# A mixture-of-experts kernel: two 64-row remainder units with raw fp32 weights in place of two 128-row units with split weights

## The chip, the cores and the metric

The kernel runs on one core of a Trainium2 chip. The metric is the time of one execution on the device in microseconds (us); the median of 3 runs before is 899.38 us. The engines are named as in the profile: PE (matmul), PEld (PE's weight loads), DVE (vector), ACT (scalar), POOL (GpSimd) and SP (which issues most DMAs).

## What is computed

Attention over 4 x 448 rows of 12 heads of 64, then two mixture-of-experts layers over the 1792 rows of 768. Each layer sends every row to one of 8 experts and multiplies it by that expert's two matrices, in fp32:

```
for e in range(E):                       # E = 8
    mask = e_idx == e                    # argmax of the gate's logits
    if not mask.any():
        continue
    h = np.maximum(x[mask] @ w1[e], 0.0) # 768 x 1024
    out[mask] = gate_w[mask, None] * (h @ w2[e])   # 1024 x 768
```

## The kernel before, in words

The work of a layer is cut into units: some rows of one expert, with a fixed capacity. The second layer is e2, e3, then four units of up to 304 rows in `seq` (B0 to B3, the list `S["B"]`), then two remainder units of up to 128 rows, S0 and S1 (`S["S"]`). Which expert and which rows a unit has is worked out on the device: `table2` and `table3` fill entries, `M.reg` loads them into registers. An expert gets a further 304-row unit while more than 128 rows are left (the threshold `thr`), and a remainder unit for what is left then. If there are more units than these, a branch (`others`, in the middle of B3) does them; it also runs for no unit, and then costs only its test.

A unit is `unit` and `halves` (from line 373). The first half has KF=8 blocks of 128 hidden columns with KD=6 weight tiles of 128x128 each, the second half KD=6 blocks with KF=8 tiles each. Full precision comes from split planes: an fp32 weight `r1[k]` or `r2[k]` becomes an fp16 high plane (`w1h`, `w2h`, a cast on ACT, L294) and a bf16 low plane (`w1l`, `w2l`, a subtraction on DVE, L295). The rows are split in the same way (`xsplit`, L340 and L341) and transposed by DMA (`xtrans`, L344). `mm3` (L357) then issues three matmuls per weight tile; the middle one takes its width from a register (`width`, at least 32), so the profile writes it as 128x0:

```
for (ah,al,bh,bl) in pairs:
    for o,a,b in ((p,ah,bh),(s(p),ah,s(bl)),(p,al,bh)):
        self.nc.tensor.matmul(o,a,b,start=i==0,stop=i==tot-1); i+=1
```

The relu makes `hh` (ACT, L360) and `hl` (DVE, L361). The second half's results are copied (L424), transposed on PE (`ytrans`, L414), multiplied by the gate (DVE, L415) and scattered to the output by POOL (L366); the last block's are done at the start of the next unit (`post`).

The work for later units is woven in. At step 0 the unit fetches the payload (row numbers and gates) of the unit after next, at step 7 its rows (a gather on POOL, L336). In the first half `split_w2` makes this unit's w2 planes. At step 7.5 the next unit's w2 is loaded into `r2`. In the second half `warm2` splits the next unit's w1, and behind it `bring` loads the w1 of the unit after next into `r1`. `XPLAN` says when the next unit's rows are split and transposed. The program order of each engine is pinned (`pin`).

Of the kernel before, what the change touches and what calls it, by code (L numbers as in the profile page):

```python
# [27 lines left out]
class Moe:  # L28
# [287 lines left out]
    def fetch_pay(self,u,slot=None):  # L316
        nc=self.nc
        if slot is None: u.slot=self.slot; self.slot=(self.slot+1)%4
        s=self.reg(u.ent,u.g,1,E*NT-1)
        pay=self.pays[u.slot]; N=u.N; ordt=u.L.ord  # L320
        FT=N//128; rem=N-FT*128
        nc.sync.dma_start(out=pay[:,:FT,:],in_=ordt[ds(s,FT*128),:].rearrange("(t p) w -> p t w",p=128))
# [9 lines left out]
    def gather(self,u,t=None):  # L332
        nc=self.nc; ntl=u.ntl; idx=self.idxs[u.slot]
        for t in range(ntl) if t is None else (t,):
            m=u.rows[t]
            nc.gpsimd.indirect_dma_start(out=self.xr[t][:m],out_offset=None,in_=u.L.src[0:u.nrow,:],in_offset=bass.IndirectOffsetOnAxis(ap=idx[:m,t:t+1],axis=0),bounds_check=u.nrow-1,oob_is_err=False)  # L336
    def xsplit(self,u,t,eng=None,part=2):

        nc=self.nc; m=u.rows[t]; x=self.xr[t][:m]; h=self.XS[:m,t,0]
# [33 lines left out]
    def unit(self,u,nx=None,fx=None,side=None,late=0,mid=None,fast={},now=False,fp=0,fr=7,**kw):  # L373

        gen=self.gen(); side=dict(side or {})
        plan=XPLAN[late] if nx is not None else {}
        def do(s):
            if fx is not None and s==fp: self.fetch_pay(fx)
            for k,t in plan.get(s,()):
                if t<nx.ntl:  # L380
                    if k=="t": self.xtrans(nx,t)
                    else: self.xsplit(nx,t,self.nc.gpsimd if k=="p" else None)
            if fx is not None and s==fr: self.fetch_rows(fx)
            for _ in range(fast.get(s,1)): next(gen,None)
            for f in side.pop(s,()): f()  # L385
        warm=nx is not None and not nx.same
        for _ in self.halves(u,nx,warm,do,fx,cut=mid is not None,**kw): mid([k for s in plan if s<MID for k in plan[s]])
        for _ in gen: pass
        for s in sorted(side): do(s)
        if now:  # L390
            self.flush()
            if fx is not None: self.fetch_idx(fx)
        elif fx is not None and fr>KF+KD: self.fetch_rows(fx)
    def halves(self,u,nx,warm,do,fx=None,early=True,wfb=None,gp=0,cut=False):
# [17 lines left out]
        def ytrans(d):  # L412
            q=self.pt.tile([128,4,128],F32,name="pty",tag="pt")[:,:ntl]
            for t in range(ntl): nc.tensor.transpose(q[:,t,:],self.yt[:,d,ts(t,128)],self.ident)  # L414
            nc.vector.tensor_tensor(out=self.yr[:,:ntl,ts(d,128)],in0=q,in1=bc(pay[:,:ntl,1:2],[128,ntl,128]),op=ALU.mult)  # L415
        Y={}
        def after(d):
            ytrans(d)
            if u.L.nxt is not None:
                for j in range(2): nc.tensor.matmul(self.lgp[:2*E,:N],u.L.nxt["wgs"][:,d],Y.pop((d,j)),start=(d,j)==(0,0),stop=(d,j)==(KD-1,1))  # L420
        for db in range(KD):
            p=self.ps.tile([128,512],F32,name="pl2",tag="pl")[:,:N]
            self.mm3(p,[(self.w2h[:,k,ts(db,128)],self.w2l[:,k,ts(db,128)],hh[:,k],hl[:,k]) for k in range(KF)],r)
            nc.scalar.copy(self.yt[:,db,:N],p)  # L424
            if u.L.nxt is not None:
                yh,yl=[self.st.tile([128,self.NM],F32R,name=n,bufs=2)[:,:N] for n in ("yh","yl")]
                nc.scalar.copy(yh,p); nc.vector.tensor_tensor(out=yl,in0=p,in1=yh.bitcast(F32),op=ALU.subtract)
                Y[db,0],Y[db,1]=yh,yl
            if db>0: after(db-1)
            if warm: self.warm2(db,None)  # L430
            do(KF+db)
        if fx is not None and early and not fx.same: self.bring(fx)
        def post():
# [2 lines left out]
            if u.L.nxt is not None: yield from self.route2(u,pay[:,:ntl,1:2])  # L436
            yield
        self.post=post
    def redo(self,u,nx,fx,turn,done):
        u.e=None; self.fetch(u,u.slot); self.cold(u); self.xall(u)  # L440
        self.turn=turn-1; next(self.halves(u,None,False,lambda s: None,cut=True))
        if nx is None: return
        self.fetch(nx,nx.slot)
        for k,t in done:
            if t<nx.ntl: (self.xtrans if k=="t" else self.xsplit)(nx,t)
# [25 lines left out]
    2:{7.5:[("s",0),("s",1),("s",2),("t",0),("t",1),("t",2)]},None:{10:[("s",0),("t",0)]}}  # L471
class LazyUnit:
    def __init__(self,S,*key,same=False):
        object.__setattr__(self,"_k",(S,key)); object.__setattr__(self,"same",same)
    def _u(self):
        o,key=object.__getattribute__(self,"_k")
        for k in key: o=o[k]
# [6 lines left out]
class Layer:  # L484
    def __init__(self,w1,w2,src,dst,ordt,nxt=None): self.w1,self.w2,self.src,self.dst,self.ord,self.nxt=w1,w2,src,dst,ordt,nxt
class Unit:
    def __init__(self,L,ent,g,N,same=False):
        self.L,self.ent,self.g,self.N,self.same=L,ent,g,N,same
        self.ntl=(N+127)//128; self.rows=[min(128,N-t*128) for t in range(self.ntl)]; self.e=None; self.slot=None; self.nrow=NT; self.w1=False

# [311 lines left out]
def body_full(tc,q,k,v,g_q,g_k,wg,wog,w1,w2,mod,wg2,bias2,v1,v2,out,stop=False,O=None):  # L802
    nc=tc.nc
    with ExitStack() as ctx:
# [145 lines left out]
        def table2():  # L950
            c,off=cc2,off2; M.reduce_counts(tp,c2,lp,tag="tp",out=c)
            rem=lp.tile([128,E],F32,name="rem"); nc.vector.tensor_tensor(out=rem,in0=c,in1=off,op=ALU.subtract)
            M.nchunks(lp,rem,N2,128,out=nb)
            yield
            yield from M.chunks(S["b2"],lp,nb,off,c,N2,G2)
        def table3():
# [5 lines left out]
            yield from M.chunks(S["s2"],lp,ns,off3,c,128,E)  # L962
# [71 lines left out]
```

## Time and profile before

| | |
|---|---|
| median of 3 runs | 899.38 us (899.12 to 903.18) |
| the profiled execution | 898.82 us |
| its span, first to last instruction | 897.0 us |
| PE busy | 831.3 us, 93% |
| DVE busy | 682.4 us, 76% |
| ACT busy | 527.1 us, 59% |
| mean granted clock of PE | 0.978 |

Busy time is the share of the span in which an engine works; a busy PE need not be PE at its peak. The granted clock is a share of 2.4 GHz, and 0.50 is the lower of its two levels, 1.2 GHz. Times in the rows are counted from the span's start.

### The profile page before, as it was taken

To read this page: it belongs to the slowest core of one execution; us is meant where nothing else is said; L and a number is where in the kernel's file an instruction comes from. 1 tells how busy PE (TensorE), PEld (TensorE's weight loads), DVE (VectorE), ACT (ScalarE), POOL (GpSimd) and SP (SyncE) were. 2 spreads that over 40 slices of the span, in tenths; PEclk is the share of its full clock that TensorE was granted. 3 is DMA by queue.
4 is the path that set the end of the run, shared out by engine and by line. 5 is a ranking of instruction groups with operands and counts; after the bars stand their busy time and mean duration, and the time that the engine had idled before them with its cause. 6 is when DMAs were issued, how large, how long until landed. Compare 5 with 4: busy or idle time off the path is not lost. (4 is left out here: it accounts for less than half of the span.)

```text
span 897.0 us, 23334 instructions
## 1 busy us (share of the span) xinstructions
PE 831.3 (93%) x8881; PEld 652.1 (73%) x8898; DVE 682.4 (76%) x1417; ACT 527.1 (59%) x967; POOL 384.1 (43%) x406
## 2 busy tenths in 40 slices
PE   4699999998899799799999999989999999999986
PEld 1366666665565588677889899888777778876776
DVE  6688889888879875776787888888766667654585
ACT  4577776776667652555555566565545545544473
POOL 5686777776776521321423422434113415312020
PEclk9799999999999899999999999999999999999999
DMA  5578665665566472989487687779677595965671
GB/s 133 126 162 194 154 155 166 167 163 150 128 168 156 120 218 56 275 295 332 94 307 209 219 324 218 246 284 303 189 295 205 205 309 150 331 175 210 218 244 55
DMA packets 143931, 181.84 MB, mean 203 GB/s; under 512 B 73737, under 2 KB 111385, under 8 KB 143809
## 3 DMA queue, kind: packets, MB, share of 16 engines
q1 hardware_dynamic: 135712, 157.45, 59.6%
q0 software_dynamic: 6784, 22.32, 7.8%
q8 instruction: 72, 1.18, 0.6%
q10 hardware_dynamic: 1312, 0.47, 0.2%
q14 instruction: 51, 0.41, 0.2%
HBM read 130.12 MB, written 24.33 MB: 172 GB/s over the span
## 5 line engine op out<-in xcount | busy, mean ns | idle before, releaser
L357 PE MATMUL pl<-XT,w1h 128*128 128x304 f16 (+7 forms) x1620 | 250.3, 263 | 5.4 <-PEq L986 2.2
L357 PE MATMUL pl<-hh,w2h 128*128 128x304 f16 (+7 forms) x816 | 209.6, 269 | 0.2
L357 PE MATMUL pl<-hh,w2l 128*128 128x304 f16 (+7 forms) x816 | 209.2, 268 | 0.0
L357 PE MATMUL pl<-XT,w1l 128*128 128x304 f16 (+7 forms) x810 | 207.8, 269 | 1.3 <-DVE w1l L295 1.3
L357 PE MATMUL pl<-hl,w2h 128*128 128x0 bf16 x816 | 202.6, 255 | 3.3 <-DVE hl L361 3.2
L357 PEld LDWEIGHTS <-w1h 128*128 128x128 f16 x1632 | 149.2, 98 | 29.8 <-issue 6.2
L357 PEld LDWEIGHTS <-w2h 128*128 128x128 f16 x1632 | 148.9, 98 | 24.9 <-issue 1.8
L648 POOL TENSOR_TENSOR plo<-p 128x448 f16<-128x448 f32 x142 | 139.3, 1001 | 50.2 <-ACT p L645 46.8
L295 DVE TENSOR_TENSOR w1l<-r,w1h 128x1024 bf16<-128x1024 f32 x96 | 118.1, 1245 | 37.8 <-ACT w1h L294 37.7
L424 ACT COPY yt<-pl 128x304 f32<-128x304 f32 (+7 forms) x102 | 37.2, 364 | 139.1 <-PE pl L357 138.9
L341 POOL TENSOR_TENSOR XS<-xr,XS 128x768 bf16<-128x768 f32 (+5 forms) x27 | 47.3, 1771 | 165.4 <-ACT XS L340 165.4
L294 ACT CAST w1h<-r 128x1024 f16<-128x1024 f32 x96 | 99.6, 1054 | 0.1
L645 ACT ACTIVATE p<-pst,eb 128x896 f32<-128x896 f32 (+1 forms) x96 | 86.5, 911 | 14.4 <-PE pst L641 13.4
L357 PEld LDWEIGHTS <-w2l 128*128 128x128 bf16 x816 | 80.1, 98 | 17.2 <-issue 4.4
L360 ACT ACTIVATE hh<-pl 128x304 f16<-128x304 f32 (+7 forms) x135 | 50.2, 373 | 71.6 <-PE pl L357 64.1
L658 PE MATMUL av<-vv,p 128*128 128x65 f16 (+1 forms) x768 | 89.7, 199 | 2.0 <-ACT xrow L670 2.0
L357 PEld LDWEIGHTS <-w1l 128*128 128x128 bf16 x816 | 80.1, 98 | 14.7 <-DVE w1l L295 1.6
L658 PEld LDWEIGHTS <-p 128*128 128x128 bf16 (+1 forms) x768 | 73.5, 102 | 21.0 <-issue 15.0
L660 PE MATMUL av<-vv,plo 128*128 128x65 f16 (+1 forms) x768 | 87.9, 196 | 0.6 <-DVE plo L648 0.6
L659 PE MATMUL av<-vv,p 128*128 128x64 f16 (+1 forms) x768 | 88.4, 198 | 0.0
L622 DVE TENSOR_REDUCE m<-psm 128x2 f16<-128x896 f32 x70 | 76.0, 1085 | 8.3 <-PE psm L617 6.7
L295 DVE TENSOR_TENSOR w2l<-raw,w2h 128x768 bf16<-128x768 f32 x64 | 73.1, 1142 | 8.4 <-ACT w2h L294 8.2
(314 smaller groups left out, 1661.5 us busy)
## 6 DMA issues: line engine op xcount, KB each, us to landing
r<-in_moe_w_dram SPq DMA_DIRECT2D x96, 512.0 KB, 9.0
raw<-in_moe_w_dram SPq DMA_DIRECT2D x64, 384.0 KB, 5.9
r2a<-in_moe_w_dram SPq DMA_DIRECT2D x32, 384.0 KB, 7.3
r2b<-in_moe_w_dram SPq DMA_DIRECT2D x32, 384.0 KB, 7.7
T<-Z SPq DMA_DIRECT2D x48, 224.0 KB, 3.2
T<-Z SPq DMA_DIRECT2D x48, 112.0 KB, 3.1
yd<-zero SPq DMA_DIRECT2D x14, 384.0 KB, 3.3
rv<-in_v_dram SPq DMA_DIRECT2D x24, 192.0 KB, 3.8
```

The source lines that it names most:

```text
L294: if part!=1: nc.scalar.copy(h,t)
L295: if part!=0: (eng or nc.vector).tensor_tensor(out=l,in0=t,in1=h,op=ALU.subtract)
L341: if part!=0: (eng or nc.vector).tensor_tensor(out=self.XS[:m,t,1].bitcast(BF16),in0=x,in1=h,op=ALU.subtract)
L357: self.nc.tensor.matmul(o,a,b,start=i==0,stop=i==tot-1); i+=1
L360: nc.scalar.activation(h,p,AF.Relu)
L424: nc.scalar.copy(self.yt[:,db,:N],p)
L622: if t<3: nc.vector.tensor_reduce(m[:,t:t+4:3],p[:,:,:S],axis=AX.X,op=ALU.max,negate=True)
L645: self.nc.scalar.activation(self.d["P",i][:,self.u(kt)],p[:,:nn,:S],AF.Exp,bias=self.eb,scale=0.125)
L648: eng.tensor_tensor(out=self.d["L",i][:,u],in0=P[:,u],in1=self.hi(P)[:,u],op=ALU.subtract)
L658: nc.tensor.matmul(o,hh,w[:,0:65],start=kt==0,stop=False)
L659: nc.tensor.matmul(o[:,0:64],hh,w[:,65:129],start=False,stop=False)
L660: nc.tensor.matmul(o,ll,w[:,0:65],start=False,stop=kt==3)
```

## The change

The two remainder units hold NS=64 rows in place of 128, and the threshold for a further 304-row unit falls from 128 to 64. They run in a new function, `unit32`: one matmul per weight tile, with the raw fp32 weights and the fp32 rows, 64 columns wide; no planes, no register for the width. S0 reads its weights from `r1` and `r2`. S1 has buffers of its own: `x1` is new, `x2` is a view of the planes of w1, which are not read any more when it is loaded. S1's w1 is loaded during B1, its w2 during B3. The rows are transposed on PE (`xtrans32`) in place of the DMA. `ytrans` becomes a method.

```diff
+    def alloc_f32(self,st,n):
+        self.x1=[st.tile([128,F],F32,name=f"x1_{i}") for i in range(KD)]
+        self.x2=[t[:,i].bitcast(F32) for t in (...) for i in range(2)]
+        self.xt32=st.tile([128,KD,n],F32,name="xt32"); self.hh32=st.tile([128,KF,n],F32,name="hh32")
...
-        plan=XPLAN[late] if nx is not None else {}
+        plan=XPLAN[late] if nx is not None and not nx.f32 else {}
...
-            if warm: self.warm2(db,None)
+            if warm and not nx.f32: self.warm2(db,None)
...
+    def xtrans32(self,u):
+        nc=self.nc; m=u.rows[0]
+        q=self.pt.tile([128,4,128],F32,name="ptx",tag="pt")...
+        for k in range(KD): nc.tensor.transpose(q[:,k],self.xr[u.x0][:m,ts(k,128)],self.ident[:m,:m])
+        nc.vector.tensor_copy(self.xt32,q)
+    def unit32(self,u,w1,w2,side={}):
+        nc=self.nc; N=u.N; gen=self.gen()
+        def do(s):
+            next(gen,None)
+            for f in side.get(s,()): f()
+        for fb in range(KF):
+            p=self.ps.tile([128,512],F32,name="pl1",tag="pl")[:,:N]
+            for k in range(KD): nc.tensor.matmul(p,w1[k][:,ts(fb,128)],self.xt32[:,k],start=k==0,stop=k==KD-1)
+            do(fb)
+            nc.scalar.activation(self.hh32[:,fb],p,AF.Relu)
+        for db in range(KD):
+            p=self.ps.tile([128,512],F32,name="pl2",tag="pl")[:,:N]
+            for k in range(KF): nc.tensor.matmul(p,w2[k][:,ts(db,128)],self.hh32[:,k],start=k==0,stop=k==KF-1)
+            nc.scalar.copy(self.yt[:,db,:N],p)
+            if db>0: self.ytrans(u,db-1)
+            do(KF+db)
+        def post():
+            self.ytrans(u,KD-1); self.scatter(u)
+            yield
+        self.post=post
...
-            M.set_caps(CAPS,((128,0),(N2,128),(N2,0)))
+            M.set_caps(CAPS,((128,0),(N2,NS),(N2,0)))
...
-        S["B"]=[Unit(L2,be,g,N2) for g in range(G2)]; S["S"]=[Unit(L2,se,g,128) for g in range(E)]
+        S["B"]=[Unit(L2,be,g,N2) for g in range(G2)]; S["S"]=[Unit(L2,se,g,NS,f32=True,x0=g) for g in range(2)]
...
-        sides={0:{KF+i:[stepper("table3")] for i in range(6)},1:{2:[more]},2:{1:[known]},5:{2:[nc.gpsimd.drain]}}
+        def x1(a,b):
+            M.expert(s1)
+            for k in range(a,b): M.load_w(M.x1,L2.w1,s1.e,k)
+            s1.w1=True; s1.e=None
+        def x2():
+            M.expert(s1)
+            for k in range(KF): M.load_w(M.x2,L2.w2,s1.e,k)
+        sides={0:{KF+i:[stepper("table3")] for i in range(6)},1:{2:[more],4:[lambda: x1(0,3)],6:[lambda: x1(3,6)]},2:{1:[known]},3:{8:[x2],9:[lambda: M.xtrans32(s0)]}}
         for j,u in enumerate(seq):
-            nx,fx=seq[j+1] if j<5 else None,seq[j+2] if j<4 else None
+            nx,fx=(seq+[s0,s1])[j+1:j+3]
             M.unit(u,nx=nx,fx=fx,side=sides.get(j),late=0,mid=others(u,nx,fx) if j==3 else None)
+        M.unit32(s0,M.r1,M.r2,{KF:[lambda: M.xtrans32(s1)]})
+        M.unit32(s1,M.x1,M.x2,{2:[nc.gpsimd.drain]})
```

**PE, where B3 ends and S0 begins.** `pl` is the sum in PSUM, `pty` the transposed results, `XT` the transposed rows, `r_0` to `r_5` the tiles of `r1`. Before:

```order
L357 MATMUL pl_27302<-hh,w2l 128x304
L414 MATMUL pty<-ident,yt 128x128 x3
L350 TENSOR_LOAD s2gw
L350 ISA x2
L351 ISA
L357 LDWEIGHTS w1h
L357 MATMUL pl_27364<-XT,w1h 128x128
L357 LDWEIGHTS w1h
L357 MATMUL pl_27364<-XT,w1h 128x128
L357 LDWEIGHTS w1l
L357 MATMUL pl_27364<-XT,w1l 128x128
```

And with the change:

```order
L361 MATMUL pl_27345<-hh,w2l 128x304
L442 MATMUL pty<-ident,yt 128x128 x3
L456 MATMUL pl_27376<-xt_5621,r_0_70 128x64
L456 MATMUL pl_27376<-xt_5621,r_1_71 128x64
L456 MATMUL pl_27376<-xt_5621,r_2_72 128x64
L456 MATMUL pl_27376<-xt_5621,r_3_73 128x64
L456 MATMUL pl_27376<-xt_5621,r_4_74 128x64
L456 MATMUL pl_27376<-xt_5621,r_5_75 128x64
L442 MATMUL pty<-ident,yt 128x128 x3
```

Three matmuls per tile, each with a weight load of its own, become one fp32 matmul, for which the program holds no separate load; the load of the width goes.

**SP, in B1, between the payload fetch for B3 and the input transposes for B2.** `x_0` to `x_5` are the tiles of `x1`. Before:

```order
L323 DMA pay_83<-o_1128 48x4
L344 DMA_TRANSPOSE XT<-XS 128x12x128 x2
L344 DMA_TRANSPOSE XT<-XS 128x12x48
L298 ISA
L298 DMA raw_114<-in_moe_w_dram 128x768
```

And with the change:

```order
L327 DMA pay_83<-o_1128 48x4
L306 TENSOR_LOAD s2gi
L306 ISA x2
L302 ISA
L302 DMA x_0_5615<-in_moe_w_dram 128x1024
L302 ISA
L302 DMA x_1_5616<-in_moe_w_dram 128x1024
L302 ISA
L302 DMA x_2_5617<-in_moe_w_dram 128x1024
...
L302 DMA x_5_5620<-in_moe_w_dram 128x1024
L348 DMA_TRANSPOSE XT<-XS 128x12x128 x2
```

Six loads of 512 KB and two loads of a register stand ahead of the transposes.

**DVE, from B3's second half into S0.** `yr` are the rows to scatter, `xt` is `xt32`. Before:

```order
L295 TENSOR_TENSOR w2l<-raw_114,w2h 128x768
L415 TENSOR_TENSOR yr<-pty,pay_83 128x3x128
L361 SCALAR_TENSOR_TENSOR hl<-pl_27364,hh 128x128
L295 TENSOR_TENSOR w2l<-raw_114,w2h 128x768
L361 SCALAR_TENSOR_TENSOR hl<-pl_27403,hh 128x128
```

And all that DVE has from there to the end with the change:

```order
L443 TENSOR_TENSOR yr<-pty,pay_83 128x3x128
L448 COPY xt_5621<-ptx 128x384
L443 TENSOR_TENSOR yr<-pty,pay_83 128x3x128 x5
L448 COPY xt_5621<-ptx 128x384
L443 TENSOR_TENSOR yr<-pty,pay_84 128x128 x6
L443 TENSOR_TENSOR yr<-pty,pay_81 128x128 x6
```

The subtractions for the low planes are gone; two copies of transposed rows come in.

## Rows read from the trace of the kernel before

**Rows 1.** The page, section 1: PE's busy time.

```profile
PE 831.3 (93%) x8881; PEld 652.1 (73%) x8898; DVE 682.4 (76%) x1417; ACT 527.1 (59%) x967; POOL 384.1 (43%) x406
```

**Rows 2.** Busy time by stretch: B3, S0, S1; last PEclk, DMA share, GB/s.

```profile
813.50:855.60 42.10, 39.90 (x301) 30.21 (x300) 21.58 (x31) 17.24 (x29) 5.87 (x5) 0.96 0.56 199
855.60:875.90 20.30, 16.77 (x316) 15.33 (x315) 18.05 (x29) 16.24 (x31) 5.09 (x4) 1.00 0.73 229
875.90:891.80 15.90, 14.34 (x278) 13.33 (x278) 10.57 (x24) 8.41 (x21) 0.97 (x1) 1.00 0.10 35
```

**Rows 3.** Waits of PE from 855.7 to 891.2: total, times, longest, us.

```profile
PE pl L357 <- DVE hl L361: 2.3, 3, 0.8
```

**Rows 4.** Groups by shape, DVE, 855.7 to 891.2: busy us, mean ns.

```profile
L295 DVE TENSOR_TENSOR w2l<-raw,w2h 128x768 bf16<-128x768 f32 x8 | 8.3, 1039 | 0.4 <-ACT w2h L294 0.3
L295 DVE TENSOR_TENSOR w1l<-r,w1h 128x1024 bf16<-128x1024 f32 x6 | 7.2, 1218 | 1.6 <-ACT w1h L294 1.6
```

**Rows 5.** Timeline of PE, start of S0: start us, us, instruction, count.

```profile
855.39 0.49 PE L414 MATMUL pty<-ident,yt 128*128 128x128 f32 x3
855.72 0.23 PE L357 MATMUL pl<-XT,w1h 128*128 128x128 f16 x2
855.80 0.22 PE L357 MATMUL pl<-XT,w1l 128*128 128x128 f16 x1
...
856.54 0.28 PE L414 MATMUL pty<-ident,yt 128*128 128x128 f32 x1
```

**Rows 6.** Timeline of PE, end of S1.

```profile
891.04 0.22 PE L357 MATMUL pl<-hh,w2h 128*128 128x128 f16 x1
891.10 0.19 PE L357 MATMUL pl<-hl,w2h 128*128 128x0 bf16 x1
891.12 0.22 PE L357 MATMUL pl<-hh,w2l 128*128 128x128 f16 x1
891.18 0.28 PE L414 MATMUL pty<-ident,yt 128*128 128x128 f32 x1
```

**Rows 7.** Groups by shape, whole span: the fp32 matmuls of the gate logits.

```profile
L679 PE MATMUL psm<-wgt,xt 128*128 128x16 f32 x176 | 23.3, 264 | 0.7 <-ACT xt L676 0.7
L679 PE MATMUL lg<-wgt,xt 128*128 128x16 f32 x16 | 2.0, 259 | 0.1
L679 PEld LDWEIGHTS psm<-wgt,xt 128*128 128x128 f32 x176 | 21.5, 191 | 5.5 <-issue 4.4 <-ACT xt L676 0.9
```

**Rows 8.** Timeline of PEld: bursts of fp32 weight loads.

```profile
324.17 0.97 PEld L679 LDWEIGHTS lg<-wgt,xt 128*128 128x128 f32 x8 [0.20 <-ACT xt L676]
464.37 0.74 PEld L455 LDWEIGHTS lg<-fold,lt 16*128 16x128 f32 x6 [0.20 <-issue]
```

**Rows 9.** Timeline of PE in B3, behind the branch; in brackets the idle time before.

```profile
829.31 0.41 PE L357 MATMUL pl<-XT,w1h 128*128 128x304 f16 x2 [2.20 <-PEq L986]
...
829.69 0.42 PE L357 MATMUL pl<-XT,w1h 128*128 128x304 f16 x2
...
830.12 0.71 PE L357 MATMUL pl<-XT,w1h 128*128 128x304 f16 x2
...
830.88 0.71 PE L357 MATMUL pl<-XT,w1h 128*128 128x304 f16 x2
```

**Rows 10.** Timeline of SP's queue: B1's input transposes, and S0's w2 in B3.

```profile
755.26 6.50 SPq L344 DMA_TRANSPOSE XT<-XS  x3
...
838.72 2.13 SPq L298 DMA_DIRECT2D raw<-in_moe_w_dram  x4
```

**Rows 11.** Stretches in B1: PE busy, PEclk, DMA share, GB/s.

```profile
739.00:743.00 4.00, 4.00 (x37) 1.00 1.02 406
743.00:748.00 5.00, 5.00 (x45) 1.00 0.18 56
748.00:752.00 4.00, 4.00 (x37) 1.00 0.37 147
```

**Rows 12.** A stretch of B3, columns as in rows 2: the granted clock.

```profile
830.00:833.40 3.40, 3.40 (x16) 2.00 (x15) 1.99 (x3) 0.80 (x2) 0.00 (x0) 0.50 0.00 0
```

More of the change, by code (lines that the diff above doesn't have):

```diff
@@ L287, in alloc_state @@
         self.yr=rp.tile([128,ntl,D],F32,name="yr",tag="xt")
+    def alloc_f32(self,st,n):
+        self.x1=[st.tile([128,F],F32,name=f"x1_{i}") for i in range(KD)]
+        self.x2=[t[:,i].bitcast(F32) for t in (self.w1h.rearrange("p (a b) f -> p a (b f)",a=2)[:,:,:2*D],self.w1l.rearrange("p (a b) f -> p a (b f)",a=2)[:,:,:2*D],self.w1h.rearrange("p (a b) f -> p a (b f)",a=2)[:,:,2*D:],self.w1l.rearrange("p (a b) f -> p a (b f)",a=2)[:,:,2*D:]) for i in range(2)]
+        self.xt32=st.tile([128,KD,n],F32,name="xt32"); self.hh32=st.tile([128,KF,n],F32,name="hh32")
     def alloc_psum(self,ctx,sm):
@@ L321, in fetch_pay @@
         FT=N//128; rem=N-FT*128
-        nc.sync.dma_start(out=pay[:,:FT,:],in_=ordt[ds(s,FT*128),:].rearrange("(t p) w -> p t w",p=128))
+        if FT: nc.sync.dma_start(out=pay[:,:FT,:],in_=ordt[ds(s,FT*128),:].rearrange("(t p) w -> p t w",p=128))
         if rem: nc.sync.dma_start(out=pay[:rem,FT,:],in_=ordt[ds(s+FT*128,rem),:])
@@ L335, in gather @@
             m=u.rows[t]
-            nc.gpsimd.indirect_dma_start(out=self.xr[t][:m],out_offset=None,in_=u.L.src[0:u.nrow,:],in_offset=bass.IndirectOffsetOnAxis(ap=idx[:m,t:t+1],axis=0),bounds_check=u.nrow-1,oob_is_err=False)
+            nc.gpsimd.indirect_dma_start(out=self.xr[t+u.x0][:m],out_offset=None,in_=u.L.src[0:u.nrow,:],in_offset=bass.IndirectOffsetOnAxis(ap=idx[:m,t:t+1],axis=0),bounds_check=u.nrow-1,oob_is_err=False)
     def xsplit(self,u,t,eng=None,part=2):
@@ L411, in halves @@
         if warm: self.expert(nx); w2s()
[L412 to L415, printed above, removed]
         Y={}
         def after(d):
-            ytrans(d)
+            self.ytrans(u,d)
             if u.L.nxt is not None:
@@ L438, in halves, with ytrans @@
         self.post=post
+    def ytrans(self,u,d):
+        nc=self.nc; ntl=u.ntl
+        q=self.pt.tile([128,4,128],F32,name="pty",tag="pt")[:,:ntl]
+        for t in range(ntl): nc.tensor.transpose(q[:,t,:],self.yt[:,d,ts(t,128)],self.ident)
+        nc.vector.tensor_tensor(out=self.yr[:,:ntl,ts(d,128)],in0=q,in1=bc(self.pays[u.slot][:,:ntl,1:2],[128,ntl,128]),op=ALU.mult)
+    def xtrans32(self,u):
+        nc=self.nc; m=u.rows[0]
+        q=self.pt.tile([128,4,128],F32,name="ptx",tag="pt").rearrange("p a b -> p (a b)")[:,:KD*u.N].rearrange("p (k n) -> p k n",k=KD)
+        for k in range(KD): nc.tensor.transpose(q[:,k],self.xr[u.x0][:m,ts(k,128)],self.ident[:m,:m])
[20 more added lines that the diff above has]
+        self.post=post
     def redo(self,u,nx,fx,turn,done):
@@ L444, in redo @@
         for k,t in done:
-            if t<nx.ntl: (self.xtrans if k=="t" else self.xsplit)(nx,t)
+            if t<nx.ntl and not nx.f32: (self.xtrans if k=="t" else self.xsplit)(nx,t)
         if nx.w1: nx.e=None; nx.w1=False; self.bring(nx)
@@ L473, in __init__ @@
     def __init__(self,S,*key,same=False):
-        object.__setattr__(self,"_k",(S,key)); object.__setattr__(self,"same",same)
+        object.__setattr__(self,"_k",(S,key)); object.__setattr__(self,"same",same); object.__setattr__(self,"f32",False)
     def _u(self):
@@ L486, with __init__ @@
 class Unit:
-    def __init__(self,L,ent,g,N,same=False):
-        self.L,self.ent,self.g,self.N,self.same=L,ent,g,N,same
+    def __init__(self,L,ent,g,N,same=False,f32=False,x0=0):
+        self.L,self.ent,self.g,self.N,self.same,self.f32,self.x0=L,ent,g,N,same,f32,x0
         self.ntl=(N+127)//128; self.rows=[min(128,N-t*128) for t in range(self.ntl)]; self.e=None; self.slot=None; self.nrow=NT; self.w1=False
@@ L792, in run @@
             else: self.do(n,i)
-N2=304; NE=240; CAPS=(304,288,256,240,224,208,192); G1=14; G2=10; G4=13; MID=5
+N2=304; NE=240; CAPS=(304,288,256,240,224,208,192); G1=14; G2=10; G4=13; NS=64; MID=5
 EXT={"rb0":20.47730,"ra0":20.51363,"ra1":20.63295,"ra2":20.66887,"ra3":20.75474,"ra4":20.84877,"ra5":20.84945,"ra6":20.85224,"ra7":20.85231,"ra8":20.85245,"rk0":20.96677,"rs0":21.04675,
@@ L896, in body_full @@
         if stop: return pin(tc,mark)
-        wp2=ctx.enter_context(tc.tile_pool(name="wp2",bufs=1)); M.more_w2(wp2,rp); M.alloc_state(wp2,rp)
+        wp2=ctx.enter_context(tc.tile_pool(name="wp2",bufs=1)); M.more_w2(wp2,rp); M.alloc_state(wp2,rp); M.alloc_f32(wp2,NS)
         M.alloc_psum(ctx,tp)
@@ L952, in table2 @@
             rem=lp.tile([128,E],F32,name="rem"); nc.vector.tensor_tensor(out=rem,in0=c,in1=off,op=ALU.subtract)
-            M.nchunks(lp,rem,N2,128,out=nb)
+            M.nchunks(lp,rem,N2,NS,out=nb)
             yield
@@ L961, in table3 @@
             yield
-            yield from M.chunks(S["s2"],lp,ns,off3,c,128,E)
+            yield from M.chunks(S["s2"],lp,ns,off3,c,NS,E)
         F.update(table2=table2,table3=table3)
@@ L966, in body_full @@
         M.unit(e3,nx=B0,fx=S["B"][1],side={0:[lambda: M.fetch_pay(B0)],2:[lambda: M.fetch_rows(B0)]},late=1,fp=8,fr=9)
-        seq=S["B"][:4]+S["S"][:2]
+        seq=S["B"][:4]; s0,s1=S["S"]
         (be,nbi),(se,nsi)=S["b2"],S["s2"]
```

## The prediction

> **What bounds the kernel now.** I read the page first. PE is busy for 93% of the span [rows 1], so the question for any stage is whether PE waits there and for whom. The next view is the table of stages around the change [rows 2]. B3 is the last 304-row unit (813.5 to 855.6), S0 and S1 are the two remainder units. In B3 PE is busy 39.90 of 42.10 us, in S0 16.77 of 20.30, in S1 14.34 of 15.90. So PE bounds the tail, with some waiting in S0. The longest wait of PE's matmuls in the stretch of S0 and S1 [rows 3] names the cause: DVE, which makes the low planes. The groups of DVE there [rows 4] show why: six w1 planes at 1218 ns and sixteen w2 planes, eight of them at 1039 ns, have to be made inside 35 us.
>
> The timeline of PE at the start of S0 [rows 5] gives the price of one 128x128 weight tile now. From 855.72 to 856.54 PE runs six tiles, each as three matmuls: 0.82 us / 6 = **0.137 us per tile**. The last rows of S1 [rows 6] show the same triple as about 0.055, 0.025 and 0.055 us: the middle one, whose width comes from a register (128x0), costs half of a 128-column one. So the remainders hold at most about 64 rows.
>
> **What the change does to PE.** The stretch to replace runs from S0's first matmul at 855.72 [rows 5] to the transpose right behind S1's last matmul at 891.18 [rows 6]: 35.46 us. Each unit has 8x6 + 6x8 = 96 weight tiles.
>
> - Old content: 192 tiles x 0.137 = 26.3 us; 14 transposes of results (3 of B3, 6 of S0, 5 of S1) at 0.11 (three from 855.39 to 855.72 [rows 5]) = 1.5 us; what is left, 35.46 - 27.8 = **7.7 us, is PE waiting** for planes. That is all that removing the splits can give back.
> - New content: one fp32 matmul of 64 columns per tile. The trace of before has fp32 matmuls with fp32 weights of 128x128 in the gate logits (L679). The source issues 4 per block in 24 blocks, 96 in all; the profile has 176 + 16 = 192 matmul records and as many weight loads [rows 7]. So each fp32 matmul runs as two loads and two matmuls. Eight loads in a row take 0.97 us, and the last one alone about 0.19 [rows 7, 8]: (0.97 - 0.19) / 7 = 0.111 us per load, **0.223 us per fp32 matmul**.
> - 192 x 0.223 = 42.8 us. The same 14 transposes stay, 6 transposes of S1's rows are added (they run in S0): 20 x 0.11 = 2.2 us. S0's own 6 input transposes come at the end of B3, where PE has no slack: 0.65 us. Sum 45.65 us.
>
> Difference on PE: 45.65 - 35.46 = **+10.2 us**. Put another way: 192 tiles cost 0.086 us more each (+16.5), 12 transposes come in (+1.3), and 7.7 us of waiting goes.
>
> Whether 64 columns cost more than the 16 of L679 is what the trace does not show. The 8-column fp32 matmuls of L455 have the same step, (0.74 - 0.19) / 5 = 0.11 us [rows 8], so the load sets it and the columns lie under it. Fp32 transposes move 128 columns at 0.109 us each [rows 5]. Lower end: 0.109 per pass, 41.9 us, 0.9 less than my sum. Upper end: the stream is added to the load, and each pass streams its 64 columns twice, which is 128 columns at 0.055 [rows 6]: 0.111 + 0.055 = 0.166 per pass, 63.7 us, 21 more. I take 0.1115, the row that has the same instruction.
>
> On the number of passes the Trainium skill says otherwise. Its page "FP8 and Floating Point Precision", TensorE Precision Notes, says that a true fp32 product takes four passes through the array. By four loads per matmul at the row's 0.111 the estimate would be 42.8 us more, some 952 us. The count of records speaks against four loads; the page's four products fit if each of the two matmuls streams its columns twice, which is the upper end above.
>
> **The end.** From 891.18 to 897.0 the chain is copy, transpose, multiply, scatter (L424, L414, L415, L366). It stays, with 64 instead of 128 columns in one copy: 0.1 us less at most.
>
> **DVE and ACT.** In S0 and S1 22 weight splits, 16 `hl` planes and the casts go; what replaces them (relus of 64 columns, copies of 64 columns, two copies of 128x384) is small. They come out at nothing beyond the 7.7 us already counted, because PE covers them. In B3's second half the six w1 splits go too; PE did not wait for them there (its only idle stretch in B3 is the 2.20 us at 829.31 [rows 9]), so nothing.
>
> **The moved loads.** S1's w1 (6 x 512 KB) moves into B1, on SP's queue behind the payload fetch and ahead of the input transposes, which are issued at 755.26 [rows 10]. The DMA engines are full until 743, and then 0.18 and 0.37 busy until 752 [rows 11]; 3.1 MB at 406 GB/s need 7.7 us. They fit and cost nothing. Were they late, the transposes behind them would slip by up to 8 us; those are issued in the middle of a unit and wanted at the start of the next, half of some 42 us later [rows 2]. S1's w2 (8 x 384 KB) goes into the planes of w1 as soon as B3's first layer has been multiplied, behind S0's w2 on SP. That is 6.3 MB, 15.5 us at 406 GB/s from 838.72 [rows 10], done near 855 and wanted in S1's second half, 30 us later. Nothing stands behind them on SP. The gather of S1's rows comes earlier in the program, in B3, into a buffer of its own.
>
> **Sum.** 898.82 us (the profiled execution) + 10.2 - 0.1 = 908.9. The median of the runs is 0.56 us above that execution, so I write **909.0 us**, slower by 1.1%. A measurement of this kernel can tell about 0.5%, 4.5 us, from no change.
>
> **The rivals.**
>
> *B: the stream is not hidden under the load.* A pass then costs 0.14 (64 columns once, 0.028) to 0.166 us. For: no row has fp32 passes of more than 16 columns. Against: 8 and 16 columns cost the same. Price: 384 x 0.028 to 0.055 = 11 to 21 us, 920 to 930 us.
>
> *C: the clock falls.* The granted clock was 0.50 from 830.0 to 833.4 after PE had stood idle for 2.20 us [rows 9, 12]; at that level the f16 triple took 830.12 to 830.88, 0.76 us, against 0.38 just before (829.31 to 829.69). In the fp32 units PE would spend most of a pass on loading. If that is taken for idleness, the 45.65 us double: up to 955 us, less if only a part of the stretch is hit. For: it has no row against it, since the longest fp32 burst is under 2 us. Against: the fall that the rows show came after a wait of PE, and in the new units it never waits. By the Trainium skill, "TensorE: Matmul & The Clock Gate", Part 1, activity keeps the clock up; by that rule C does not happen, and the fall at 830 agrees, but no run here shows what weight loads count for.
>
> *D: not slower.* If an fp32 matmul of this shape needs its pair of loads only once, 0.111 us per tile, the 192 tiles take 21.4 us and the time is 887.5 us. The point that decides is 0.170 us per tile (0.223 less 10.2 / 192): below it the lost waiting outweighs the slower matmuls. For: 7.7 us of waiting do go. Against: two records per matmul in every burst [rows 7].
>
> *E: it does not do what it says.* A remainder of 65 to 128 rows would now become a further 304-row unit, and a fifth one runs in the rarely taken branch. A warm unit of that size takes 42.1 us [rows 2], so 941 us or more. The half-width middle matmul [rows 6] speaks against it in S1; in S0 the pair of 855.72 ends its turn at 855.80, 0.08 us, which says the same [rows 5].
>
> **How the numbers follow.** My forecast 0.67, B 0.13, C 0.14, D 0.05, E 0.01. The range has to hold 8 in 10, so it takes my forecast and B: from 905 (the lower end of the pass price, and 3 us for waits that I count and that may hide) to 930. Outside stay C, E and D, 0.20. My forecast, B, C and E make 0.95, of which I put 0.01 within 0.5% for waits in B3 that go unseen: slower by over 0.5% is 0.94. D is faster by over 0.5% with 0.04, and lies within 0.5% with 0.01, where the price comes out near 0.170: within 0.5% is 0.02.
>
> **What would show it.** In the profile of the changed kernel: 384 matmul records with fp32 weights of 64 columns, stepping by 0.11 us; PE without a gap from the end of B3 to the last transpose; S0 and S1 of some 22.5 us each; granted clock 1.00 there; DVE and ACT mostly idle; the last scatter near 903 us; B0 to B3 as long as before. I am wrong if the step is 0.14 or more (B), if the clock is 0.50 there (C), if there is one record per matmul (D), or if B2 or B3 start late (the moved loads).

## The result, and the profile after

The changed kernel takes 913.19 us (median of 4 runs, 911.26 to 915.31), the kernel before, run beside it, 900.17 us (899.12 to 903.18): a ratio of 1.014, 95% interval 1.0103 to 1.0176. It is slower, by more than the 0.5% that a measurement can tell, and inside the range forecast; 909.0 was forecast. The execution that was profiled took 914.38 us, with a span of 912.7 us, 15.7 us more than the span of before.

The first row to read is PE's busy time on the page, beside [rows 1].

```profile
PE 849.2 (93%) x8701; PEld 669.1 (73%) x8716; DVE 653.9 (72%) x1375; ACT 502.2 (55%) x937; POOL 381.2 (42%) x404
```

PE is busy for 17.9 us more, with 180 instructions fewer; DVE lost 28.5 us of work. The next view is the table of stages, with the columns of [rows 2]: B3, S0 and S1 of the changed kernel.

```profile
820.28:862.37 42.09, 40.05 (x303) 30.26 (x302) 14.76 (x25) 10.50 (x20) 4.25 (x4) 0.96 0.58 201
862.37:885.10 22.73, 22.73 (x209) 22.59 (x208) 2.84 (x7) 3.26 (x14) 2.87 (x3) 1.00 0.12 42
885.10:906.90 21.80, 21.80 (x201) 21.80 (x199) 1.75 (x6) 3.06 (x14) 0.93 (x1) 1.00 0.01 3
```

In S0 and S1 PE is busy for all of the time, PEld for nearly all of it, DVE for 4.6 us in 44.5; the granted clock is 1.00, the higher level. The waits of PE from 820 to 908 (total, times, longest, us) say the same: one wait in B3, at the branch, as in [rows 9], a short one for the last copy, and none of the waits for DVE that [rows 3] has.

```profile
PE pl L361 <- PEq L1016: 2.0, 1, 2.0
PE pty L442 <- ACT yt L462: 0.2, 1, 0.2
```

What fills PE is in the groups by shape of that stretch (columns as in [rows 4]), here the first layer, then the transposes of S1's rows.

```profile
L456 PE MATMUL pl<-xt,r 128*128 128x64 f32 x96 | 10.9, 274 | 0.0
L456 PE MATMUL pl<-xt,x 128*128 128x64 f32 x96 | 10.9, 274 | 0.0
L456 PEld LDWEIGHTS pl<-xt,r 128*128 128x128 f32 x96 | 10.9, 192 | 0.0
...
L447 PE MATMUL ptx<-ident,xr 64*128 64x64 f32 x6 | 0.6, 230 | 0.0
```

A unit has 48 tiles in the first layer, and here are 96 matmuls and 96 weight loads for each: two passes per fp32 matmul, as in L679 before [rows 7]. The ends of the stretch, in PE's timeline (columns as in [rows 5]), have the price of one:

```profile
862.17 0.49 PE L442 MATMUL pty<-ident,yt 128*128 128x128 f32 x3
862.50 0.89 PE L456 MATMUL pl<-xt,r 128*128 128x64 f32 x7
...
906.45 0.61 PE L461 MATMUL pl<-hh,w1l 128*128 128x64 f32 x4
906.89 0.28 PE L442 MATMUL pty<-ident,yt 128*128 128x128 f32 x1
```

Four passes take 0.61 us, of which the last alone is 0.27: (0.61 - 0.27) / 3 = 0.11 us per pass, the step of [rows 8]. From S0's first matmul to the transpose behind S1's last: 906.89 - 862.50 = 44.39 us, against 35.46 before [rows 5, 6]: +8.93. From there to the end of the span it is 5.8 us, as before. So the tail accounts for some 9 of the 15.7 us. The rest was there before S0 began, 6.78 us later than in the profile of before. To see where, I cut both traces at the first unit of the first layer, at the start of e2 and at B3's first matmul, which lies some 1 us ahead of where the tables above cut B3 (columns as in [rows 2]). Before:

```profile
0.00:320.89 320.89, 281.56 (x3549) 186.29 (x3551) 266.43 (x456) 220.28 (x396) 218.70 (x269) 0.96 0.62 154
320.89:619.37 298.48, 284.30 (x2898) 254.65 (x2907) 234.77 (x637) 166.96 (x333) 95.65 (x84) 0.99 0.76 238
619.37:812.75 193.38, 193.38 (x1541) 151.57 (x1545) 130.14 (x243) 97.24 (x159) 56.86 (x42) 1.00 0.75 245
```

And with the change:

```profile
0.00:323.15 323.15, 283.08 (x3548) 186.10 (x3550) 268.79 (x456) 220.20 (x396) 218.43 (x269) 0.95 0.62 152
323.15:625.71 302.56, 286.41 (x2898) 255.49 (x2907) 234.73 (x637) 166.84 (x333) 97.42 (x84) 0.99 0.76 237
625.71:819.08 193.37, 193.37 (x1541) 151.70 (x1545) 129.79 (x243) 97.01 (x159) 56.33 (x42) 1.00 0.79 258
```

The attention takes 2.26 us more and the first layer 4.08 us more, with the same numbers of PE instructions within one. The stretch that holds the moved loads of `x1` (e2 to B2) is as long as before, 193.37 against 193.38, and PE never stops in it. B3 is 0.45 us longer (819.08 to 862.50, against 812.75 to 855.72). The account of the span closes: 6.33 + 0.45 + 8.93 = 15.71 us.

B3's 0.45 us are two things. Its second layer, from its first matmul to S0's, has the transposes of S0's rows; here it is before, then with the change, and then these transposes in PE's timeline:

```profile
835.60:855.72 20.12, 20.12 (x162) 15.83 (x161) 10.28 (x14) 8.28 (x13) 1.05 (x1) 1.00 0.88 311
841.76:862.50 20.74, 20.74 (x168) 16.23 (x165) 3.73 (x10) 2.56 (x7) 0.97 (x1) 1.00 0.68 250
```

```profile
847.92 0.49 PE L442 MATMUL pty<-ident,yt 128*128 128x128 f32 x3
848.34 0.58 PE L447 MATMUL ptx<-ident,xr 64*128 64x64 f32 x6
848.86 0.30 PE L361 MATMUL pl<-hh,w2h 128*128 128x304 f16 x1
```

The second layer is 0.62 us longer with six more instructions. The first layer is 0.17 us shorter, since the wait at the branch is 2.0 us in place of 2.2 [rows 9], and that is no part of the change. So the change costs 0.62 + 8.93 = 9.55 us in B3, S0 and S1.

Two theories stand. **Theory 1**: the change costs the 9.55 us of B3, S0 and S1, and the 6.33 us ahead of them differ from one execution to the next whatever the kernel. **Theory 2**: something of the change acts there too, for example its buffers, which move others. Behind them stand the rivals on the price of a pass (stream, clock), and the question whether the planes could have been kept at less cost.

### The profile page after: what moved, and what is told of

The parts are those of the page before. It is cut to its first block, busy times and chain, and to the rows that moved or that the text cites. A ratio compares the mean times of both kernels' runs of the same rounds, so it can differ in the third digit from the quotient of the medians.

```text
span 912.7 us, 22840 instructions
## 1 busy us (share of the span) xinstructions
PE 849.2 (93%) x8701; PEld 669.1 (73%) x8716; DVE 653.9 (72%) x1375; ACT 502.2 (55%) x937; POOL 381.2 (42%) x404
## 5 line engine op out<-in xcount | busy, mean ns | idle before, releaser
L361 PE MATMUL pl<-XT,w1h 128*128 128x0 bf16 (+8 forms) x1428 | 237.9, 273 | 4.8 <-PEq L1016 2.0
L361 PE MATMUL pl<-XT,w1l 128*128 128x304 f16 (+7 forms) x714 | 195.5, 278 | 0.3 <-issue 0.3
L361 PE MATMUL pl<-hh,w2h 128*128 128x304 f16 (+7 forms) x720 | 194.3, 275 | 0.0
L361 PE MATMUL pl<-hh,w2l 128*128 128x304 f16 (+7 forms) x720 | 193.8, 274 | 0.0
L361 PE MATMUL pl<-hl,w2h 128*128 128x0 bf16 x720 | 187.8, 264 | 1.8 <-DVE hl L365 1.8
L361 PEld LDWEIGHTS <-w2h 128*128 128x128 f16 x1440 | 134.1, 98 | 24.2 <-issue 1.4
L299 DVE TENSOR_TENSOR w1l<-r,w1h 128x1024 bf16<-128x1024 f32 x84 | 104.5, 1259 | 31.7 <-ACT w1h L298 29.4
L424 ACT COPY yt<-pl 128x304 f32<-128x304 f32 (+7 forms) x90 | 33.8, 376 | 139.8 <-PE pl L361 130.6
L443 DVE TENSOR_TENSOR yr<-pty,pay 128x384 f32<-128x384 f32 (+2 forms) x102 | 46.7, 458 | 63.5 <-PE pty L442 62.4
L298 ACT CAST w1h<-r 128x1024 f16<-128x1024 f32 x84 | 87.2, 1054 | 0.1
L370 POOL DMA_INDIRECT out_dram<-yr,idx x20 | 23.1, 1157 | 141.2 <-DVE yr L443 99.9
```

Source lines behind the costliest of these rows:

```text
L298: if part!=1: nc.scalar.copy(h,t)
L299: if part!=0: (eng or nc.vector).tensor_tensor(out=l,in0=t,in1=h,op=ALU.subtract)
```

## The experiments

**again**: the changed kernel without any edit, in more runs.

> The changed kernel once more, beside the kernel before. In the first profile of it the two fp32 units took 44.4 us against 35.5, but S0 also began 6.8 us later, and only 0.7 us of that is the six transposes put into B3. Theory 1 (chance): the other 6 us come from where the granted clock fell in the attention part and the first layer, which differs from run to run. Then S0 begins somewhere from 855 to 862 us this time, the fp32 stretch is 44.4 us again, and the ratio over five rounds is 1.010 to 1.013. Theory 2 (the new buffers or the moved instructions slow the earlier stages): S0 begins at 862 again and the ratio stays at 1.014 or above.

Measured: 909.72 us (5 runs, 908.22 to 911.19) against 899.38 (23 runs): ratio 1.0105 (1.0079 to 1.0131). Its S0 and S1 (table of stages) and their ends (timeline of PE):

```profile
858.74:881.40 22.66, 22.66 (x208) 22.53 (x207) 2.84 (x7) 3.27 (x14) 2.87 (x3) 1.00 0.12 42
881.40:903.20 21.80, 21.80 (x200) 21.80 (x200) 1.75 (x6) 3.07 (x14) 0.93 (x1) 1.00 0.01 3
```

```profile
858.84 1.00 PE L456 MATMUL pl<-xt,r 128*128 128x64 f32 x8
...
903.24 0.28 PE L442 MATMUL pty<-ident,yt 128*128 128x128 f32 x1
```

The stretch is 44.40 us, to 0.01 us the one of the first profile, but S0 starts at 858.84 in place of 862.50. B3's second layer (838.11 to 858.84) takes 20.73 us, as in the first profile. So the 9.55 us repeat, and the time ahead of them doesn't. The ratio is worth 7.1 to 11.8 us, which leaves at most some 2 us for anything else of the change.

**alloc**: the kernel before, with the new buffers allocated and nothing else.

```diff
...
-        ...; M.more_w2(wp2,rp); M.alloc_state(wp2,rp)
+        ...; M.more_w2(wp2,rp); M.alloc_state(wp2,rp); M.alloc_f32(wp2,64)
```

> The kernel before, with the four new buffers allocated and nothing else. Theory 1: no difference, ratio 1.000 within 0.003. Theory 2 (the place of the buffers slows the earlier stages): ratio 1.003 to 1.007 and S0 begins 2 to 6 us later than 855.7.

Measured: 900.7 us, ratio 1.0009 (0.999 to 1.0027). The stretch from S0's first matmul (856.97) to the last transpose but one (892.43) is 35.46 us, the same as before. The buffers cost nothing that this measurement can tell (by the interval at most 2.4 us), which takes away the one form of theory 2 that I could name: the moved loads run later than the difference arises.

**split64**: units of 64 rows as in the change, but with planes and three matmuls per tile.

```diff
...
-N2=304; NE=240; ...; MID=5
+N2=304; NE=240; ...; NS=64; MID=5
...
-            M.set_caps(CAPS,((128,0),(N2,128),(N2,0)))
+            M.set_caps(CAPS,((128,0),(N2,NS),(N2,0)))
...
-        ...; S["S"]=[Unit(L2,se,g,128) for g in range(E)]
+        ...; S["S"]=[Unit(L2,se,g,NS) for g in range(E)]
...
```

> The kernel before with 64-row remainder units, split planes kept (three f16 matmuls per tile, 64 columns). If DVE's subtractions set the length of S0 and S1 (22 planes at 0.94 to 1.22 us, 16 hl planes, 12 products, some 28 us), the stretch from S0's first matmul to the last transpose falls from 35.5 only to 30 to 33 us, and the time by 3 to 5 us (ratio 0.995 to 0.997). If PE's matmuls set it (192 tiles at 0.137 us, at 64 columns 0.083), it falls by 10 us (0.989). If neither, no change.

Measured: 896.4 us, ratio 0.997 (0.9953 to 0.9987). A tile is cheap where its planes are there, as the timeline of PE at S0's start shows: eleven tiles in 854.64 - 853.72 = 0.92 us, 0.084 us each, against 0.137 with 128 columns [rows 5] and 0.22 in fp32.

```profile
853.72 0.21 PE L357 MATMUL pl<-XT,w1h 128*128 128x64 f16 x2
...
854.64 0.21 PE L357 MATMUL pl<-XT,w1h 128*128 128x64 f16 x2
854.70 0.19 PE L357 MATMUL pl<-XT,w1l 128*128 128x64 f16 x1
855.52 0.21 PE L357 MATMUL pl<-XT,w1h 128*128 128x64 f16 x2 [0.63 <-DVE hl L361]
```

So 192 tiles are some 16 us of work, and yet the stretch takes 33.8 (852.86 to 886.64), more than the 30 to 33 expected from DVE's work. The two largest of PE's waits in it, and three stretches of S0 from the table of stages, tell why:

```profile
PE pl L357 <- DVE hl L361: 5.0, 10, 1.2
PE pl L357 <- DVE w1l L295: 1.6, 2, 1.1
```

```profile
852.86:857.20 4.34, 2.69 (x77) 2.49 (x75) 3.84 (x6) 4.34 (x11) 2.35 (x2) 1.00 0.44 129
857.20:860.60 3.40, 3.10 (x60) 2.77 (x60) 3.40 (x8) 2.88 (x8) 1.07 (x2) 0.50 0.29 116
860.60:870.21 9.61, 7.24 (x167) 6.47 (x165) 8.06 (x14) 7.37 (x16) 2.60 (x2) 0.82 0.76 205
```

DVE is busy for 15.30 of these 17.35 us. A w1 plane takes it 1219 ns, as before [rows 4], however few the rows, so PE waits. In the second of two waits, of 0.63 and 1.20 us, the clock falls to the lower level (0.50 from 857.2 to 860.6), and it does so three times more up to S1's end; the expectation had no such falls in it. The halved rows alone are worth 0.3%.

**col16**: the changed kernel with the fp32 matmuls 16 columns wide: only the first 16 of a unit's 64 rows go through them.

```diff
-            ...: nc.tensor.matmul(p,w1[k][:,ts(fb,128)],self.xt32[:,k],start=k==0,stop=k==KD-1)
+            ...: nc.tensor.matmul(p[:,:16],w1[k][:,ts(fb,128)],self.xt32[:,k,:16],start=k==0,stop=k==KD-1)
...
-            ...: nc.tensor.matmul(p,w2[k][:,ts(db,128)],self.hh32[:,k],start=k==0,stop=k==KF-1)
+            ...: nc.tensor.matmul(p[:,:16],w2[k][:,ts(db,128)],self.hh32[:,k,:16],start=k==0,stop=k==KF-1)
...
```

> The changed kernel with the fp32 matmuls 16 columns wide in place of 64; rows 17 to 64 of the two remainder units are left out of the computation. Load-bound theory: the step stays at 0.111 us and the fp32 stretch at 44.4 us, the time as that of the changed kernel within 1.5 us. Stream-counts theory (columns add to the step): 48 columns fewer per pass make it 0.02 to 0.04 us shorter, 8 to 15 us in all. Clock theory (the granted clock hangs on what is streamed, and weight loads count for little): with a quarter of the columns the clock falls to 0.50 in the stretch, the step doubles to 0.22 us, and the time is up to 44 us longer.

Measured: 944.62 us, ratio 1.0495 (1.0465 to 1.0525): less work, and much slower, in each of its four runs (944.50 to 946.79). The table of stages from the start of S0 on (S0 begins at 858.35):

```profile
858.00:862.20 4.20, 4.20 (x41) 4.20 (x39) 1.12 (x2) 0.78 (x3) 1.01 (x1) 1.00 0.02 4
862.20:897.80 35.60, 35.60 (x172) 35.45 (x172) 1.72 (x5) 1.96 (x11) 1.87 (x2) 0.50 0.07 26
897.80:939.20 41.40, 41.40 (x199) 41.40 (x198) 1.75 (x6) 2.50 (x14) 0.93 (x1) 0.50 0.01 1
```

4 us into S0 the clock falls to 0.50 and stays there to the end, though PE never stops. Ahead of the fall, PEld's timeline has a row of twelve loads at the higher level:

```profile
858.24 1.42 PEld L456 LDWEIGHTS pl<-xt,r 128*128 128x128 f32 x12
```

That is (1.42 - 0.19) / 11 = 0.11 us per pass, as with 64 columns: 48 columns less do not shorten it. The group of S1's first layer shows the price at the lower level:

```profile
L456 PEld LDWEIGHTS pl<-xt,x 128*128 128x128 f32 x96 | 20.7, 334 | 0.0
L456 PE MATMUL pl<-xt,x 128*128 128x16 f32 x96 | 20.5, 371 | 0.0
```

20.7 us / 96 = 0.216 us per pass, twice the 0.111 at the higher level. With 64 columns (**again**) the granted clock of the same stretch was 1.00. The Trainium skill, "TensorE: Matmul & The Clock Gate", Part 1, has the clock follow how busy PE has been. By the profile's busy time this trace does not agree: PE was busy for 4.20 of 4.20 us before the fall and for 35.60 of 35.60 us behind it, and had the lower level all the same. The measurement decides. What in the narrower matmuls made the clock fall is not shown, and no width between 16 and 64 was tried.

**col128**: the changed kernel with units of 128 rows, raw fp32 weights and 128 columns; the input rows are transposed in two pieces.

```diff
...
-N2=304; NE=240; ...; NS=64; MID=5
+N2=304; NE=240; ...; NS=128; MID=5
```

> The changed kernel with remainder units of 128 rows again, so the fp32 matmuls are 128 columns wide; the rows of S0 and S1 are transposed in two pieces of three blocks. Load-bound theory: a pass steps by 0.111 us as at 16 and 64 columns, the fp32 stretch stays within 1 us of 44.4 us, and the time is that of the changed kernel (ratio 1.009 to 1.013). If the stream is added to the load or binds at this width, a pass takes 0.14 to 0.17 us, the stretch 54 to 66 us, and the ratio is 1.022 or more.

Measured: 914.02 us, ratio 1.0141 (1.0099 to 1.0183), against 902.21 for the kernel before beside it. S0 and S1 in the table of stages, and the first layer's groups:

```profile
857.72:880.69 22.97, 22.97 (x209) 22.97 (x207) 3.31 (x8) 3.89 (x14) 2.86 (x3) 1.00 0.11 41
880.69:902.67 21.98, 21.98 (x199) 21.98 (x198) 1.75 (x6) 3.82 (x14) 0.97 (x1) 1.00 0.01 2
```

```profile
L457 PE MATMUL pl<-xt,r 128*128 128x128 f32 x96 | 11.0, 275 | 0.0
L457 PE MATMUL pl<-xt,x 128*128 128x128 f32 x96 | 11.0, 275 | 0.0
```

Twice the columns cost 0.56 us in 44.95. Loading the weights sets the step, and up to 128 columns lie under it. With raw fp32 weights, then, halving the rows saves PE next to nothing. The ratio lies just above the 1.009 to 1.013 expected, but its interval holds the 1.0105 of **again**.

**mix**: the raw fp32 weights only where planes would be late. On top of split64, S0's first layer has planes (they are made during B3), its second layer uses the raw `r2`; S1 keeps planes, made during S0 from its w2, which was loaded to a buffer of its own in B1.

```diff
...
+            if u.raw2:
+                if fb%2==0: self.split_x(fb//2)
...
+            if u.raw2:
+                for k in range(KF): nc.tensor.matmul(p,self.r2[k][:,ts(db,128)],self.hh32[:,k],start=k==0,stop=k==KF-1)
+            else: self.mm3(p,[(self.w2h[:,k,ts(db,128)],...
...
-        S["B"]=...; S["S"]=[Unit(L2,se,g,NS) for g in range(E)]
+        S["B"]=...; S["S"]=[Unit(L2,se,g,NS,raw2=g==0,pre2=g==1) for g in range(2)]
...
```

> 64-row units that use raw fp32 weights only where the planes would be late: S0's first half with planes (made in B3 as before), S0's second half raw from r2, S1 with planes throughout; S1's w2 is loaded in B1 into a buffer of its own, and its planes and those of S1's w1 are made during S0. Theory (PE's work per tile is 0.083 us with planes at 64 columns and 0.223 raw, and a plane costs only where PE waits for it): 48 x 0.223 + 144 x 0.083 = 22.7 us and some 1.5 us of transposes, so the stretch from S0's first matmul to the last transpose is 24 to 27 us against 35.5, and the ratio 0.988 to 0.991. Rival (ACT and DVE can't make 14 pairs of planes in S0's 16 us, so PE waits at S1's start): 28 to 32 us, ratio 0.992 to 0.996; the granted clock may then fall in the wait.

Measured: 895.43 us, ratio 0.9926 (0.9903 to 0.9949): faster than both kernels. The two units in the table of stages, and PE's waits in them:

```profile
859.71:875.24 15.53, 15.53 (x250) 15.51 (x249) 12.51 (x16) 12.80 (x27) 7.20 (x5) 1.00 0.43 109
875.24:888.86 13.62, 10.58 (x296) 10.31 (x293) 7.52 (x17) 4.46 (x16) 3.88 (x3) 0.87 0.03 6
```

```profile
PE pl L360 <- DVE hl L364: 2.2, 1, 2.2
PE pl L360 <- DVE w1l L298: 0.9, 1, 0.9
```

The stretch is 29.15 us. S0 runs without a gap; S1 still waits twice for DVE, and its mean clock is 0.87. That is the outcome of the rival (28 to 32 us), not of the theory (24 to 27). The gain over split64 comes from two edits at once, the raw half and the early load of S1's w2; no run separates them.

**mix2** and **mix_again**: in mix2 the planes of S1 are begun earlier (its rows in B3, one w2 plane by POOL at S0's start, the others spread over S0; the edit is shown against mix); mix_again is mix beside it.

```diff
...
-                if fb%2==0: self.split_x(fb//2)
+                for k,e in {0:((0,None),(1,nc.gpsimd)),3:((2,None),),5:((3,None),)}.get(fb,()): self.split_x(k,e)
...
+        if u.raw2: self.split_w1(0); self.split_w1(1)
...
+                if db<4: self.split_w1(db+2)
+                if db>2: self.split_x(db+1)
...
+        sides={...,3:{10:[lambda: M.xsplit(s1,0,nc.gpsimd)]},...}
```

> As mix (the first half of the first remainder unit with planes, its second half from raw fp32, the second unit with planes), but the planes of the second unit are begun earlier: its row planes in the third e unit, plane 1 of its w2 by POOL ahead of the scatters, the other planes spread over the first remainder unit. In mix PE still waited 1.05 us for a w1 plane and 2.36 us for a w2 plane, and the clock then fell for 3.4 us. If those planes only came late, PE now runs S0 in about 15.5 us and S1 in about 9 us, the stretch is 24.5 to 26.5 us (mix 29.1), and the ratio 0.987 to 0.991. Rival: ACT and VectorE are full, since the fourteen pairs of planes take as long as the first unit; then the wait only moves, the stretch stays at 28 to 29 us and the ratio at 0.992 to 0.993.

> The kernel of mix unchanged, beside mix2 on the same chip, so that a difference of some us between the two can be told. Expected: ratio 0.990 to 0.995 as before, a stretch of 28.5 to 29.5 us; if mix2 brings what it should, mix2 is 2.5 to 4.5 us below it.

Measured: mix2 895.2 us, ratio 0.9933 (0.9905 to 0.996); mix_again 895.6 us, ratio 0.9945 (0.992 to 0.997). The units of mix2 in the table of stages, and PE's one wait there:

```profile
861.60:877.17 15.57, 15.57 (x250) 15.54 (x250) 13.03 (x17) 12.64 (x26) 5.25 (x4) 1.00 0.41 108
877.17:887.79 10.62, 9.10 (x296) 8.88 (x293) 5.60 (x17) 4.16 (x16) 0.93 (x1) 1.00 0.02 6
```

```profile
PE pl L360 <- DVE hl L364: 1.5, 1, 1.5
```

The stretch shrank as expected, to 26.2 us, and the clock stays at 1.00; so the planes of mix were late and can be made in time. The expected ratio did not come: the medians differ by 0.4 us, where the stretch is 3 us shorter than in mix and 4 us shorter than in mix_again (30.2, a little over the 28.5 to 29.5 expected). A part of the reason is behind the stretch, where mix2 takes 8.3 us to the end of its span (887.79 to 896.1), mix 7.0, mix_again 5.9 and the kernel before 5.8. The `drain` on POOL that the kernel has at step 2 of S1 (in `sides`), DVE's last product and the last scatter in mix2:

```profile
L389 POOLq DRAIN  x1: 10550/10550/10550, 880.4 to 880.4; - x1
888.67 0.29 DVE L425 TENSOR_TENSOR yr<-pty,pay 128x128 f32<-128x128 f32 x1 [0.25 <-PE pty L424]
891.79 0.91 POOL L369 DMA_INDIRECT out_dram<-yr,idx  x1 [10.27 <-issue]
```

The rows to scatter are ready at 888.96, but the drain, 10.55 us long, holds POOL until 890.9, and the scatter starts at 891.79. In the kernel before, the same drain lasts 10.59 us from 877.3, which is over before DVE's last product ends at 892.41, and the scatter follows 0.3 us behind DVE. In mix the scatter starts 1.5 us behind DVE (890.03, 891.55). So a shorter S1 runs into the drain: from S0's first matmul to the end of the span mix2 takes 34.5 us, and mix and mix_again 36.2 each. Of the 3 to 4 us, 1.7 are left. A run with the drain at another place was not made.

Whether those 1.7 us are there can't be told from the medians: the twelve runs of mix2 lie between 892.12 and 902.33. Two profiles of one and the same program show where such spread comes from. B3's first matmul in the timeline of mix:

```profile
818.57 0.42 PE L360 MATMUL pl<-XT,w1h 128*128 128x304 f16 x2
```

and in that of mix_again:

```profile
813.46 0.42 PE L360 MATMUL pl<-XT,w1h 128*128 128x304 f16 x2
```

They are 5.1 us apart ahead of S0 and S1, which is nearly the 6.33 us between the first two profiles. These two ran on different chips, but one chip shows as much: alloc, split64 and **again** ran on one, and B3 starts at 815.76, 810.10 and 817.58 there, and the twelve runs of mix on one chip lie between 893.03 and 902.25. So theory 1 stands, within the 2 us or so that **again** and **alloc** leave open. Over the ten profiles the start of B3 lies between 810.10 (split64) and 820.81 (mix2). What sets it in an execution was not tried: PE's waits and the places where the clock falls lie differently each time.

## Why the prediction was right

- **Two passes per fp32 matmul, 0.1115 us each**: right, and a little dear. There are 384 matmul records, and what the transposes (below) leave of the stretch is 42.4 us, 0.110 us per pass. The four passes that the Trainium skill, "FP8 and Floating Point Precision", TensorE Precision Notes, gives for a true fp32 product are neither four loads (the estimate of some 952 us is out) nor twice the columns on top of the load (col128 shows no such cost).
- **The transposes**: right in size. Six transposes of input rows take 848.86 - 848.25 = 0.61 us (three at 0.109 from 847.92 end their turn at 848.25), and B3's second layer is 0.62 us longer; I had 0.65. In the stretch I counted 14 transposes of results, but it ends where the 14th starts, so it holds 13. The stretch is then 13 x 0.11 + 0.61 = 2.0 us of transposes in place of 2.2, and 44.39 - 2.0 = 42.4 us of passes in place of 42.8. The sum of +10.2 came out as 8.93 + 0.62 = **+9.55 us**.
- **The waiting that goes**: all of it went, as the sum takes it, since the whole old stretch of 35.46 us is replaced. Its split into 26.3 of work and 7.7 of waiting was too clean: PE was busy for 30.66 us of the stretch and idle for 4.8, so some 2.9 us of my waiting do not show as idle time. Whether they are short waits or slower tiles is not shown; the sum doesn't hang on it.
- **The end**: -0.1 forecast; 5.8 us before and after, so nothing that the rows can tell.
- **DVE, ACT and the moved loads at nothing**: right. e2 to B2 took 193.37 us against 193.38, the input transposes behind the loads of `x1` start at 761.59 against 755.26 [rows 10], later by the same 6.33 us as all else there, PE had no wait in S0 and S1 on a weight, and the wait at the branch in B3 is the old one.
- **The total**: 909.0 forecast, 913.19 measured, then 909.72 for the same kernel. My last step had a slip: 908.9 and the 0.56 us of the median make 909.5. By its interval the first ratio is worth 9.3 to 15.8 us and the second 7.1 to 11.8 us; the 9.55 us of the stages lie in both. In the profiled execution what lies above them is the time ahead of e2, which differs between executions. That the first median lies above the forecast for the same reason is likely and not shown.
- **The rivals**: B (stream on top of the load) is out by col128. C (the clock) is a real mechanism: it happened at 16 columns, for the whole rest of the kernel, and not at 64. I had given it little because the fall of [rows 12] came after a wait, and in the new units PE never waits; col16 shows a fall without one, so that reason was not enough. The forecast held because the clock stayed at 1.00 at 64 columns, and as far as my reasons went that was luck. D (one load) and E (a fifth large unit) did not come.

## What to carry to other kernels

In these runs a 128x128 weight tile in raw fp32 costs PE 0.22 us with 64 or 128 columns, and twice that with 16, where the clock fell, against 0.084 us for three 16-bit matmuls of 64 columns whose planes are ready: raw weights take work off the engines that split, and put more on PE. Use them where the planes can't be made in time, not for whole units: with one half-unit of the four in raw fp32, the halved rows and S1's w2 loaded early, the kernel came out 0.55 and 0.74% faster than before (mix_again, mix). When a last stage gets shorter, look at what else ends there: POOL's drain cost nothing before, and took a part of the gain of mix2. And cut both traces at a stage that the change can't reach before explaining a difference of totals.

## What was not expected of the hardware

- The clock fell to its lower level for 77 us while PE was busy all the time with fp32 loads and 16-column matmuls (0.216 us per pass in place of 0.111). At 64 and 128 columns it stayed at 1.00.
- One program reached the same instruction at 813.46 and at 818.57 us in two executions, on two chips; on one chip its times spread from 893.03 to 902.25.
- A drain on POOL took 10.55 to 10.91 us in each of the ten profiles, though the scatter ahead of it had landed long before (in mix2 2.3 us behind its start at 880.60, and so 8 us before the drain's end).
